# Holding three row loads back behind a transposing transfer, and rearranging one quad's rows on GpSimd

## The chip, the core and the metric

The kernel runs on one core of a Trainium2 chip. The core has TensorE (PE, matmuls), VectorE (DVE), ScalarE (ACT), GpSimd (POOL) and SyncE (SP), each with its own queue of instructions worked off in order, and 16 DMA engines that all queues of transfers share. The metric is device time in microseconds (us); lower is better. PSUM, where matmuls write, has eight banks.

## The reference

Two stages in one function. First an attention without softmax, for 8 batches, 12 heads, 448 positions and a head size of 64; then a two-layer perceptron over the 3584 rows of 768 that come out.

```
scores = q @ k^T / sqrt(64)
attn   = relu(scores)**2 / 448
x      = (attn @ v), heads side by side        # 3584 x 768
h      = x @ w_in                              # 768 x 2048
g      = max(h, 0) + alpha * min(h, 0)
out    = g @ w_out                             # 2048 x 768, float32
```

Inputs and output are float32. The kernel computes in bfloat16 with float32 sums.

## The kernel before, in words

**Tiling.** Four heads of one batch make a *quad*; there are 24, three to a batch. The 448 positions are laid out as 64 partitions by 7 chunks, and two heads share the 128 partitions. For each quad the kernel

- loads rows of q, k and v (`load_qk`, `load_v`), issued by GpSimd, which also turns float32 into bfloat16; 224 KB each as written;
- turns q and k so that the head size lies along partitions, into a tile `T`. Quads 0 to 4 do that on TensorE (`turn_pe`). From quad 5 on, `turn_dma` does: two copies rearrange the rows into a tile `perm` (L164), then SP issues a transposing transfer from `perm` to `T` (L166);
- computes scores per chunk (L178), relu on ScalarE (L187) or VectorE (L189), the square, mostly on VectorE (L197), and the product with v (`attnv`, L207), which ScalarE (L217) and VectorE (L218) scale into `xT`.

For each batch `f1` multiplies `xT` by w_in (L241, 16 blocks of 128 columns); ScalarE and VectorE apply the slope (L249, L250) into `gT`, which holds two batches. `f2` multiplies `gT` by w_out (L266) for one block of rows and either the first 256 or the last 512 columns, ScalarE copies the result out of PSUM (L268) and SP stores it (L274). `load_w_out(1)` loads w_out's last 512 columns in four quarters.

**Order.** All of it is written out by hand: each engine gets its instructions in the order in which the program makes the calls, and the framework adds the waits that the data needs. What matters around the change:

- *GpSimd's queue* issues all loads. At most eight of its transfers are under way, as they share eight semaphores. The stretch concerned, L374 to L380, is: rows of quad 6, q of quad 7, a 1x1 copy into `landed` that reads quad 5's `T` and so waits for its transposing transfer, k of quad 7, rows of quad 8, w_out's four quarters, v of quad 6.
- *SP's queue* issues the stores and the transposing transfers.
- *VectorE's queue* has the perm copies of quad 6 (`turn_dma(6)`, L389) after a run of squares and before the relu of quad 5's scores.
- *Buffers*: rows of q and of k, three each; `perm`, two; `T`, four; `gT`, one for two batches. Quads 5 and 7 use one `perm` buffer, 6 and 8 the other. Quad 9's rows come into the buffers of quad 6's.

After quad 4's scores TensorE's order is: `f2(0,0,0)`, scores of quad 4, `attnv(3)`, scores, `f2(0,1,0)`, `f2(0,2,0)`, scores of quad 5 (L396, the first readers of quad 5's `T`), `attnv(4)`, scores, then `f1` of batch 1 with `attnv(5)` inside it. Quad 6's scores come after `f1` of batch 1 and `f2(0,3,0)`.

Of the kernel before, what the change touches and what calls it, by code (L numbers as in the profile page):

```python
# [20 lines left out]
def kernel(  # L21
# [10 lines left out]
    nc = tc.nc  # L32
# [30 lines left out]
    landed = singles.tile([1, 1], BF16)  # L63
# [22 lines left out]
    def take_bank():  # L86
        i = min(range(8), key=lambda i: (taken[i], i))
        take(i, 1)
        return psum[:, i]


    raw, vraw = {}, {}

    def load_qk(n, names="qk"):
        b, g = divmod(n, NG)
        for name in names:
            src = q if name == "q" else k
            t = raw_pool.tile([128, 2, NJ, D], BF16, tag=name, name=f"{name}raw")
            flat = src[b].rearrange("(m two) (pp j) d -> (two pp) m (j d)", two=2, j=NJ)
            nc.gpsimd.dma_start(out=t.rearrange("p m j d -> p m (j d)"), in_=flat[:, 2 * g:2 * g + 2])  # L100
            raw[(n, name)] = t

    def load_v(n):
        b, g = divmod(n, NG)
        t = v_pool.tile([128, 2, NJ, D], BF16, tag="v", name="vraw")
        flat = v[b].rearrange("(m two) (pp j) d -> (two pp) m (j d)", two=2, j=NJ)
        nc.gpsimd.dma_start(out=t.rearrange("p m j d -> p m (j d)"), in_=flat[:, 2 * g:2 * g + 2])  # L107
        vraw[n] = t
# [11 lines left out]
    def load_w_out(h, lo=0, hi=KF, step=4):  # L120
        for lo in range(lo, hi, step):
            nc.gpsimd.dma_start(out=w_out_sb[h][:, lo:lo + step], in_=w_out_v[:, lo:lo + step, COLS[h][0]:COLS[h][1]])
# [24 lines left out]
    T = {}  # L147
# [10 lines left out]
            copy = nc.vector.tensor_copy if eng == "D" else nc.scalar.copy  # L158
            copy(dst, ps[:, 128 * lo:128 * hi])  # L159

    def turn_dma(n):
        p = perm_pool.tile([128, 2, NJ, 2, D], BF16, tag="perm", name="perm")
        for i, name in enumerate("qk"):
            nc.vector.tensor_copy(p[:, i], raw.pop((n, name)).rearrange("p s j d -> p j s d"))  # L164
        t = T_pool.tile([128, 2, NJ, 128], BF16, tag="T", name="T")
        nc.sync.dma_start_transpose(out=t.rearrange("p a j c -> p (a j) c"),  # L166
                                    in_=p.rearrange("p a j s d -> p (a j s d)"))
        T[n] = t
# [4 lines left out]
    def score_mm(n, j):  # L173
        ps = take_pair()
        t = T[n]
        for r in range(2):
            for c in range(2):
                nc.tensor.matmul(ps[64 * c:64 * c + 64, r, :S],  # L178
                                 t[64 * r:64 * r + 64, 1, j, 64 * c:64 * c + 64],
                                 t[64 * r:64 * r + 64, 0, :, 64 * c:64 * c + 64],  # L180
                                 start=True, stop=True)
        return ps

    def relu(ps, eng):
        rl = rl_pool.tile([128, 2, S], BF16, tag="rl", name="rl")
        if eng == "A":
            nc.scalar.activation(rl, ps[:, :, :S], ACTF.Relu)  # L187
        else:
            nc.vector.tensor_scalar(rl, ps[:, :, :S], 0.0, None, ALU.max)  # L189
        return rl  # L190
# [31 lines left out]
    def sc(chunks):  # L222

        for n, j, eng in chunks:
            late.append((n, j, relu(score_mm(n, j), eng)))

    def sq(k=99, eng="D"):
        for g in late[:k]:
            square(*g, eng)
        del late[:k]  # L230
# [28 lines left out]
    def f2(sb, c, h, parts=None):  # L259

        first_col, width = COLS[h][0], COLS[h][1] - COLS[h][0]
        o = o_pool.tile([128, d_model - CUT], F32, tag="o", name="osb")
        for lo, hi in parts or ((0, width),):
            ps = take_bank()[:, :hi - lo]
            for ff in range(KF):
                nc.tensor.matmul(ps, gT[sb][:, ff, bass.ts(c, 128)], w_out_sb[h][:, ff, lo:hi],  # L266
                                 start=(ff == 0), stop=(ff == KF - 1))
            nc.scalar.copy(o[:, lo:hi], ps)  # L268
            for u in range(2):
                blk = 2 * c + u  # L270
                b, j = 2 * sb + blk // NJ, blk % NJ
                rows = out[b * S:(b + 1) * S].rearrange("(pp j) d -> j pp d", j=NJ)
                eng = nc.scalar if u and parts else nc.sync
                eng.dma_start(out=rows[j][:, first_col + lo:first_col + hi], in_=o[64 * u:64 * u + 64, lo:hi])  # L274
# [4 lines left out]
    def ch(n, lo, hi, p=pat):  # L279
        return [(n, j, p[j]) for j in range(lo, hi)]  # L280
# [61 lines left out]
    def f1s(b, lo, hi):  # L342
        for ff in range(lo, hi):
            f1(b, ff)
# [6 lines left out]
    def prepare(n):  # L351
        if n < NQ:
            turn_dma(n)
        load(n + 2)
# [11 lines left out]
    f1s(0, 10, 12)  # L366
    sc(ch(3, 6, 7) + ch(4, 0, 2, "AA"))
    turn_dma(5)
    f1s(0, 12, 13)
    kept = late[:]  # L370
    del late[:]
    f1s(0, 13, 16)
    late += kept
    load_qk(6)  # L374
    load_qk(7, "q")
    nc.gpsimd.tensor_copy(landed, T[5][:1, 0, 0, :1])
    load_qk(7, "k")
    load_qk(8)
    load_w_out(1)
    load_v(6)  # L380
    f2(0, 0, 0)
# [4 lines left out]
    sq(3)  # L386
    sq(2, "A")
    sq()
    turn_dma(6)  # L389
    load_qk(9)  # L390
    load_v(7)
    load_v(8)
    load_v(9)
    f2(0, 1, 0)
    f2(0, 2, 0)
    sc(ch(5, 0, 3))  # L396
    sq(1)
    attnv(4)
# [117 lines left out]
```

## Time and profile before

| | |
|---|---|
| median of 7 runs | 386.25 us |
| lowest to highest | 386.09 to 387.46 us |
| the profiled execution | 387.46 us, of it 385.4 us span |
| PE busy | 375.3 us, 97% of the span |
| DVE busy | 266.4 us, 69% |
| ACT busy | 206.9 us, 54% |
| POOL busy | 67.9 us, 18% |
| transposing transfers, issue to landing | 19, median 6.6 us, 4.0 to 19.1 us |
| rows of q, issue to landing | 23, median 6.0 us |

The span runs from the first to the last instruction of the program in one profiled execution; the time is what the device reports around it. A busy share is of the span. A row of the timeline gives the start, the time from the first start to the last end of the merged instructions, the engine, the line of the kernel and the operation, what is written and read (`out<-in`) with partitions x elements, and in brackets how long the engine had been idle and what ended that. In a group's row the numbers after the bar are busy us, mean ns of one instruction and idle us just before. In the chain of waits each piece has its start, its length and what the time was spent on; a DMA's piece there is its whole flight. A row of DMA queues has packets, MB moved and the share of 16 engines' time. Engines named with a q (SPq) are seen while they issue.

### The profile page before, as it was taken

How to read it: one execution, taken by the hardware profiler on the slowest of the kernel's cores; microseconds unless marked ns; L12 is line 12 of the kernel's file. 1: busy time of each engine (PE TensorE's matmuls, PEld its weight loads, DVE VectorE, ACT ScalarE, POOL GpSimd, SP SyncE). 2: the span in 40 equal slices, each digit the busy share in tenths (PEclk: the TensorE clock that was granted, in tenths of full speed). 3: DMA queues.
4: the chain of work that ended last, by engine and by line, in shares of the span. 5: the costliest groups of instructions: out<-in, count | busy, mean ns of one | idle time of the engine just before them, and what ended most of it. 6: DMA issues, size and time to landing. Idle time of an engine off the chain costs nothing.

```text
span 385.4 us, 7838 instructions
## 1 busy us (share of the span) xinstructions
PE 375.3 (97%) x3178; PEld 205.9 (53%) x3200; DVE 266.4 (69%) x422; ACT 206.9 (54%) x331; POOL 67.9 (18%) x102
## 2 busy tenths in 40 slices
PE   7799999999999999999999999999999999999996
PEld 6444564555554455545465455544556445645554
DVE  3987987765768888689655897779855788526300
ACT  4977686545364664555445555637544375434321
POOL 7557325132202202022100222020000000000000
PEclk9999999999999999999999999999999999999999
DMA  9999999999992776698292972946036300120023
GB/s 159 187 204 196 201 122 212 180 194 225 177 190 47 114 129 94 111 143 110 54 161 57 146 122 42 174 66 123 21 78 95 77 0 16 43 68 2 14 68 84
DMA packets 73284, 43.42 MB, mean 113 GB/s; under 512 B 40352, under 2 KB 69792, under 8 KB 73248
## 3 DMA queue, kind: packets, MB, share of 16 engines
q0 software_dynamic: 26864, 22.45, 39.6%
q1 hardware_dynamic: 45952, 20.07, 26.8%
q8 instruction: 25, 0.41, 0.4%
q10 hardware_dynamic: 432, 0.39, 0.3%
q14 instruction: 11, 0.09, 0.1%
HBM read 45.62 MB, written 11.01 MB: 147 GB/s over the span
## 4 chain that ended last, share of the span: by engine, by line
PE 89%; DMA 6%; DVE 2%; issue 1%; ACT 0%; ACTq 0%; POOLq 0%
PE psum L266 37%; PE psum L241 36%; PE psum L178 9%; PE psum L207 7%; DMA T<-perm 3%; DMA kraw<-in_k_dram 2%; DMA qfirst<-in_q_dram 1%; DVE at L197 1%; PE psum L156 1%; DVE T L159 1%; DVE rl L189 1%; ACT osb L268 0%; ACTq L274 0%; DVE qraw L140 0%; POOLq L100 0%
## 5 line engine op out<-in xcount | busy, mean ns | idle before, releaser
L266 PE MATMUL psum<-w_out,gT 128*128 128x256 bf16 (+3 forms) x890 | 149.8, 322 | 1.2
L241 PE MATMUL psum<-xT,w_in_sb 128*128 128x448 bf16 x768 | 149.9, 353 | 0.0
L266 PEld LDWEIGHTS <-gT 128*128 128x128 bf16 x912 | 86.8, 98 | 64.2 <-issue 8.2
L241 PEld LDWEIGHTS <-w_in_sb 128*128 128x128 bf16 x768 | 73.5, 98 | 73.0 <-issue 5.5
L250 DVE SCALAR_TENSOR_TENSOR gT<-neg,beta_sb,psum 128x448 bf16<-128x448 f32 x128 | 83.6, 678 | 35.8 <-ACT neg L249 35.7
L249 ACT ACTIVATE neg<-psum 128x448 f32<-128x448 f32 x128 | 69.3, 547 | 61.4 <-PE psum L241 60.2
L187 ACT ACTIVATE rl<-psum 128x896 bf16<-128x896 f32 x113 | 97.9, 929 | 2.2 <-PE psum L178 2.2
L197 DVE TENSOR_TENSOR at<-rl 128x896 bf16<-128x896 bf16 x164 | 91.7, 619 | 0.0
L189 DVE TENSOR_SCALAR rl<-psum 128x896 bf16<-128x896 f32 x55 | 59.7, 1086 | 40.0 <-PE psum L178 39.9
L268 ACT COPY osb<-psum 128x256 f32<-128x256 f32 (+3 forms) x57 | 27.0, 473 | 104.4 <-PE psum L266 97.3
L178 PE MATMUL psum<-T 64*64 64x448 bf16 x672 | 44.7, 356 | 3.5 <-DVE T L159 1.3
L100 POOL DMA_DIRECT2D qraw<-in_q_dram x23 | 16.6, 721 | 156.9 <-DVE perm L164 148.4
L207 PE MATMUL psum<-at,vraw 64*64 64x448 bf16 x672 | 36.6, 350 | 0.3 <-DVE at L197 0.2
L178 PEld LDWEIGHTS <-T 64*64 64x64 bf16 x672 | 16.5, 106 | 22.2 <-issue 12.9
L207 PEld LDWEIGHTS <-vraw 64*64 64x64 bf16 x672 | 20.9, 106 | 12.6 <-issue 2.3
L218 DVE TENSOR_SCALAR xT<-psum 128x448 bf16<-128x448 f32 x23 | 14.4, 625 | 14.5 <-PE psum L207 10.9
L107 POOL DMA_DIRECT2D vraw<-in_v_dram x24 | 17.5, 729 | 7.5 <-DMA w_out<-in_moe_w_out_dram 4.3
L100 POOL DMA_DIRECT2D kraw<-in_k_dram x23 | 16.6, 722 | 6.4 <-DMA w_out<-in_moe_w_out_dram 3.4
L217 ACT ACTIVATE xT<-psum 128x448 bf16<-128x448 f32 x23 | 12.7, 550 | 2.6 <-PE psum L207 2.6
L164 DVE COPY perm<-qraw 128x896 bf16<-128x896 bf16 x19 | 11.7, 614 | 0.0
L164 DVE COPY perm<-kraw 128x896 bf16<-128x896 bf16 x19 | 11.6, 611 | 0.0
L117 POOL DMA_DIRECT2D w_in_sb<-in_moe_w_in_dram x16 | 10.1, 632 | 7.8 <-DMA qraw<-in_q_dram 2.3
(25 smaller groups left out, 41.9 us busy)
## 6 DMA issues: line engine op xcount, KB each, us to landing
out_dram<-osb SPq DMA_DIRECT2D x54, 128.0 KB, 2.4
vraw<-in_v_dram POOLq DMA_DIRECT2D x24, 224.0 KB, 8.1
qraw<-in_q_dram POOLq DMA_DIRECT2D x23, 224.0 KB, 6.0
kraw<-in_k_dram POOLq DMA_DIRECT2D x23, 224.0 KB, 7.1
out_dram<-osb SPq DMA_DIRECT2D x56, 64.0 KB, 2.2
w_in_sb<-in_moe_w_in_dram POOLq DMA_DIRECT2D x16, 192.0 KB, 9.0
w_out<-in_moe_w_out_dram POOLq DMA_DIRECT2D x4, 512.0 KB, 12.6
w_out<-in_moe_w_out_dram POOLq DMA_DIRECT2D x4, 256.0 KB, 8.9
```

The costliest lines, as they stand in the source:

```text
L100: nc.gpsimd.dma_start(out=t.rearrange("p m j d -> p m (j d)"), in_=flat[:, 2 * g:2 * g + 2])
L164: nc.vector.tensor_copy(p[:, i], raw.pop((n, name)).rearrange("p s j d -> p j s d"))
L178: nc.tensor.matmul(ps[64 * c:64 * c + 64, r, :S], t[64 * r:64 * r + 64, 1, j, 64 * c:64 * c + 64], t[64 * r:64 * r + 64, 0, :, 64 * c:64 * ...
L187: nc.scalar.activation(rl, ps[:, :, :S], ACTF.Relu)
L189: nc.vector.tensor_scalar(rl, ps[:, :, :S], 0.0, None, ALU.max)
L197: nc.vector.tensor_tensor(a, rl, rl, ALU.mult)
L207: nc.tensor.matmul(ps[64 * s:64 * s + 64, r, :S], vv[64 * r:64 * r + 64, s, j, :], a[64 * r:64 * r + 64, s], start=(j == 0), stop=(j == NJ ...
L241: nc.tensor.matmul(ps, w_in_sb[:, km // 2, km % 2, bass.ts(ff, 128)], xT[b][:, km // 2, km % 2, :], start=(km == 0), stop=(km == KM - 1))
L249: nc.scalar.activation(neg, ps, ACTF.Relu, scale=-1.0)
L250: nc.vector.scalar_tensor_tensor(gT[b // 2][:, ff, (b % 2) * S:(b % 2) * S + S], neg, beta_sb[:, ff:ff + 1], ps, ALU.mult, ALU.add)
L266: nc.tensor.matmul(ps, gT[sb][:, ff, bass.ts(c, 128)], w_out_sb[h][:, ff, lo:hi], start=(ff == 0), stop=(ff == KF - 1))
L268: nc.scalar.copy(o[:, lo:hi], ps)
```

## The change

The 1x1 copy that waits for quad 5's transposing transfer moves ahead of the rows of quad 6, so that the loads of q6, k6 and q7 wait too. The two copies that rearrange quad 6's rows go from VectorE to GpSimd, in its queue after the rows of quad 8 and before the four issues for w_out's last 512 columns. The issue of quad 6's transposing transfer on SP goes from before `f2(0,1,0)` to after `f2(0,2,0)`, so behind their four stores.

```diff
-    def turn_dma(n):
+    def rearrange_rows(n, eng):
         p = perm_pool.tile([128, 2, NJ, 2, D], BF16, tag="perm", name="perm")
         for i, name in enumerate("qk"):
-            nc.vector.tensor_copy(p[:, i], raw.pop((n, name)).rearrange("p s j d -> p j s d"))
+            eng.tensor_copy(p[:, i], raw.pop((n, name)).rearrange("p s j d -> p j s d"))
+        return p
+
+    def turn_dma(n, p=None):
+        p = p or rearrange_rows(n, nc.vector)
         t = T_pool.tile([128, 2, NJ, 128], BF16, tag="T", name="T")
...
     late += kept
+    nc.gpsimd.tensor_copy(landed, T[5][:1, 0, 0, :1])
     load_qk(6)
-    load_qk(7, "q")
-    nc.gpsimd.tensor_copy(landed, T[5][:1, 0, 0, :1])
-    load_qk(7, "k")
+    load_qk(7)
     load_qk(8)
+    rows6 = rearrange_rows(6, nc.gpsimd)
     load_w_out(1)
     load_v(6)
     f2(0, 0, 0)
...
     sq(2, "A")
     sq()
-    turn_dma(6)
     load_qk(9)
     load_v(7)
     load_v(8)
     load_v(9)
     f2(0, 1, 0)
     f2(0, 2, 0)
+    turn_dma(6, rows6)
     sc(ch(5, 0, 3))
```

## The prediction

> **What bounds the kernel now.** Times are us from the span's start; "T5" is the transposing transfer of quad 5, and so on; q6 and k6 are the row loads of quad 6. I read the page's chain first, then the chain in order of time, to find where TensorE isn't what ends last.
>
> ```profile
> PE 89%; DMA 6%; DVE 2%; issue 1%; ACT 0%; ACTq 0%; POOLq 0%
> ```
>
> ```profile
> 41.49 2.64 PE psum L241 x14
> 44.13 10.36 DMA T<-perm
> 54.49 0.04 issue
> 54.54 0.76 PE psum L178 x12
> ```
>
> TensorE sets the end. The chain leaves it at 44.13 for 10.36, the whole flight of T5, but that isn't what T5 costs: TensorE had other work meanwhile. Its own timeline has the price:
>
> ```profile
> 54.54 0.76 PE L178 MATMUL psum<-T 64*64 64x448 bf16 x12 [0.66 <-DMA T<-perm]
> ```
>
> It is idle from 53.88 to 54.54. After that no gap of it is longer than 0.05, so whatever is won or lost there reaches the end in full. GpSimd's timeline shows what T5 flew beside:
>
> ```profile
> 41.00 0.71 POOL L100 DMA_DIRECT2D qraw<-in_q_dram  x1 [0.83 <-PE psum L241]
> 42.13 0.71 POOL L100 DMA_DIRECT2D kraw<-in_k_dram  x1 [0.42 <-issue]
> 43.27 0.71 POOL L100 DMA_DIRECT2D qraw<-in_q_dram  x1 [0.43 <-issue]
> 54.55 0.18 POOL L376 COPY landed<-T 1x1 bf16<-1x1 bf16 x1 [10.57 <-DMA T<-perm]
> 55.03 0.72 POOL L100 DMA_DIRECT2D kraw<-in_k_dram  x1 [0.31 <-PE psum L178]
> ...
> 57.30 3.00 POOL L122 DMA_DIRECT2D w_out<-in_moe_w_out_dram  x4
> ```
>
> q6, k6 and q7 were issued just before T5; the last of them lands 10.2 after 43.27, at 53.5, and T5 at 54.5. VectorE's order just after matters for the moved copies:
>
> ```profile
> 56.24 0.61 DVE L197 TENSOR_TENSOR at<-rl 128x896 bf16<-128x896 bf16 x1
> 56.77 0.62 DVE L218 TENSOR_SCALAR xT<-psum 128x448 bf16<-128x448 f32 x1
> 57.31 1.08 DVE L189 TENSOR_SCALAR rl<-psum 128x896 bf16<-128x896 f32 x1
> 58.31 2.76 DVE L197 TENSOR_TENSOR at<-rl 128x896 bf16<-128x896 bf16 x5
> ```
>
> Here VectorE runs close ahead of TensorE. Half of quad 4's xT is ready at 57.39 and used by the fourth L241 matmul, at 56.94 + 3 x 0.2 = 57.54: 0.15 to spare. The fifth square ends at 61.07; quad 5's L207 matmuls start at 60.67 and reach it after five chunks of 0.2, at 61.67: 0.6 to spare.
>
> **What the Trainium skill says.** "SBUF — State Buffer", Who interferes with whom: GpSimd shares a pair of SBUF ports with VectorE, held for a whole instruction; a VectorE instruction with two SBUF inputs contends with a GpSimd one that reads SBUF, and who starts first makes the other wait. The squares (rl times rl) are of that kind, the L189 and L218 instructions, which read PSUM, are not. No row of before has GpSimd copying beside a square. "DMA: Bandwidth & Descriptors", Queues, rings and completion order: each DMA engine takes packets in turn from the queues that have work. The trace agrees for 76 to 82, where T7 flew beside loads, packet for packet:
>
> ```profile
> q0 software_dynamic: 1056, 0.89, 90.5%
> q1 hardware_dynamic: 1057, 0.27, 33.3%
> ```
>
> **The change, part by part.**
>
> *The three loads that now wait.* Without q6, k6 and q7 (3 x 229 KB as written, at the 201 GB/s of 36 to 50) queue 0 runs dry about 3.4 earlier. T5 then has the engines to itself sooner: 54.5 - 3.4 = 51.1; bounds 49.7 (issue 44.13 plus the 4.0 of the shortest transposing transfer, plus the rest of the older loads) and 52.5 (its slow pace when alone, 730 packets in 50.5 to 53, stays). TensorE asks at 53.88, so the wait goes: -0.66. Nothing sooner than 53.88 is to be had, TensorE is full there.
>
> *GpSimd's queue.* T5 lands at 51.3, say. Then the 1x1 copy and six issues (before: 0.48 to the first load, 0.72 to 0.85 each): 51.3 + 0.5 + 0.85 + 5 x 0.72 = 56.3. q6 lands 4.4 after its issue and k6 5.3 (q and k at 103.71 and 104.42, on idle engines): 56.2 and 57.95. So the copy of q starts at 56.3, that of k at 57.95. Their length isn't in the trace; the nearest rows:
>
> ```profile
> masks.py:199 POOL TENSOR_SCALAR_AFFINE_SELECT ident<-ident 128x128 bf16<-128x128 bf16 x1 | 0.3, 287 | 0.1
> masks.py:197 POOL MEMSET ident<- 128x128 bf16 x1 | 0.2, 204 | 0.3 <-POOLq L500 0.3
> ```
>
> Less the 93 to 95 ns of a 128x1 memset these are 0.87 and 1.5 ns per element of a partition; 896 elements on top of the 1x1 copy's 176 ns make 0.95 to 1.5, and I take 1.25. Upper bound 2.0, from the 4497 ns for 2048 elements that "GPSIMD Engine Reference", Performance versus the Vector engine, gives for a two-input add (an estimate; the same page calls one-input work nearly line-rate). The rows are done at 57.95 + 1.25 = 59.2. Behind them: w_out's four issues at 59.2 instead of 57.30. Its last quarter, issued 1.9 later, lands at 76.65 + 1.9 = 78.6 at worst (issue 59.52, 17.1 in flight before); the matmul that reads it runs at 79.80 + 12 x 0.216 - 0.66 = 81.7. Quad 9's rows, landed at 79.7 and 81.3, move to 83.2 at worst, read at 85.9. Both hidden; quads 7 and 8 land near 60 and 63 and are read at 64.6 and 72.3.
>
> *VectorE.* Two copies of 0.61 fewer, at 53.12 to 54.26. After them it waited 0.98 for TensorE, so: 0.
>
> *The shared ports.* Everything of TensorE and VectorE now runs 0.66 sooner: lone square 55.58 to 56.19, five squares from 57.65 to 60.41. The copy of q falls into the PSUM readers between. The copy of k meets the squares: if it gets between them, they end up to 1.25 later, less 0.6 to spare: 0.65. If the squares hold it off, it costs 0 and the rows come at 61.7. I take the middle: +0.3.
>
> *SP.* T6 goes behind four stores of 64 KB, issued in about 2.3 from 53.4 on, and waits for GpSimd: issue at 59.3 instead of 54.33. The stores lose T6's 1.53 ahead of them; nobody waits for them. First reader of T6: quad 6's scores, at 78.5. A nearer one: the two perm buffers alternate, so VectorE's copies for quad 8, at 72.3, need T6 landed. T6 at 59.3 has k8's tail ahead and w_out's issues beside and behind it. T11 and the like, issued between loads of the same moment, land in 6.3 (median of all 6.6): T6 at some 66 to 68. Cost: 0. T7 and T8 keep their places.
>
> Sum: -0.66 + 0.3 = -0.36. Against the profiled execution, 387.46 of which 385.4 is span, that is 387.1; I carry the difference to the median of the runs: 386.25 - 0.36 = 385.9. This kernel's runs tell about 0.2%, 0.77, from no change.
>
> **Rivals.**
>
> *The gain in full (faster).* GpSimd is held off or quick, and the T5 wait in an ordinary run is no shorter than in the profile. TensorE's idle 0.66, up to the 0.94 that its weight load waited for the same transfer: 385.3 to 385.6. Against it: the profiled run is the slowest of seven, so ordinary runs may have less of that wait.
>
> *Ports take more than T5 gives (slower).* With copies of 2.0 each, both starting ahead of squares, q is done at 58.3 and k at 60.3; the squares start 2.65 late, less 0.6: TensorE loses 2.05, net +1.4: 387.6. If T5 lands 0.7 sooner, the copy of q hits the lone square, and xT with it: up to 1.85 lost after 0.15 to spare, +1.2. It decides from copies of 1.7 each: 56.3 + 3.4 - 57.65 - 0.6 = 1.45 lost, against 0.66 won.
>
> *T6 late (slower).* If T6 shares packet for packet with w_out, as T7 did (16.5) and T8 (19.1), it lands at 75.8 or 78.4. VectorE's quad 8 copies wait, and five L250 instructions behind them (1.05 + 5 x 0.61 + 0.07 = 4.2) feed the last matmul of the next L266 group, due at 78.4: free up to a landing at 74.1, then one for one. 75.8: +1.7 - 0.36, so 387.6. Speaking for it: w_out's megabytes start at the same moment. Against: T7 and T8 met a backlog of eight loads, T6 meets the tail of one.
>
> **How the numbers follow.** Forecast 0.38 (its own range 385.4 to 386.9), full gain 0.26, ports 0.20, T6 late 0.16. The forecast lies within 0.2% but for 0.04 on the faster side: faster 0.30, same 0.34, slower 0.36. The range runs from the full gain, 385.2, to 387.8, leaving out T6 landing as late as T8 did and less than 0.1 on the fast side.
>
> **What would show it.** T5 landing by 52.5 and no idle time ahead of the first L178 after 53.8; GpSimd's two copies at 1.0 to 1.5 each; the squares after them no more than 1.25 late; T6 landed by 70 and no wait ahead of quad 8's perm copy. Wrong, if T5 isn't earlier without the three loads (its slow stretch may be its own, then the gain is 0 and the later issues stay), if a copy takes over 1.7, or if VectorE stands still near 72.

## The result, and the profile after

| | before | after |
|---|---|---|
| median | 386.31 us (35 runs, 385.78 to 387.55) | 388.26 us (14 runs, 387.17 to 389.17) |
| the profiled execution, of it span | 387.46, 385.4 | 388.61, 386.7 |

The ratio after to before is 1.0043, interval 1.0034 to 1.0053: about 1.7 us slower. The forecast was 385.9 and the range ended at 387.8; the changed kernel lies above it. It went the way of the rival "T6 late", near its price (387.6). Here and below, ratios and intervals are of runs in the faster state; one run of each of two kernels, at 392.2 and 392.3, is left out of them as over 1.5% above its kernel's fastest.

**Where the time stands now.** The page's chain of the kernel after has 3 points less of TensorE than before, one more of transfers and two more of VectorE:

```profile
PE 86%; DMA 7%; DVE 4%; issue 1%; POOL 0%; ACT 0%; ACTq 0%; DVEq 0%
```

The chain in order of time says which transfer. T5 has left it; T6 stands there with 18.32, and behind it VectorE's work comes on the path:

```profile
56.13 0.94 POOL perm L164
57.08 0.02 issue
57.09 18.32 DMA T<-perm
75.41 0.03 issue
...
75.53 1.15 DVE perm L164 x2
76.68 1.89 DVE gT L254 x4
...
78.96 0.69 DVE gT L254
79.64 0.05 issue
79.69 0.28 PE psum L270
```

(The lines of the kernel after count four higher than before's from L166 on: L254 was L250, L270 was L266.) In words: GpSimd ends the copy of k at 57.07, SP issues T6 at 57.09, T6 lands at 75.41, and only then can VectorE write quad 8's rows into the `perm` buffer that T6 read.

**The first half went better than forecast.** GpSimd's timeline after:

```profile
49.48 0.18 POOL L378 COPY landed<-T 1x1 bf16<-1x1 bf16 x1 [10.51 <-DMA T<-perm]
49.97 0.72 POOL L100 DMA_DIRECT2D qraw<-in_q_dram  x1 [0.30 <-PE psum L182]
...
54.24 0.97 POOL L164 COPY perm<-qraw 128x896 bf16<-128x896 bf16 x1
56.13 0.93 POOL L164 COPY perm<-kraw 128x896 bf16<-128x896 bf16 x1 [0.92 <-DMA kraw<-in_k_dram]
57.01 2.98 POOL L122 DMA_DIRECT2D w_out<-in_moe_w_out_dram  x4
```

T5, issued at 44.05, landed at 49.42 (it was 54.5), the two copies took 0.97 and 0.93, and w_out's issues begin at 57.01, no later than the 57.30 of before. TensorE and VectorE just after, after:

```profile
53.66 0.76 PE L182 MATMUL psum<-T 64*64 64x448 bf16 x12
```

```profile
55.37 0.62 DVE L201 TENSOR_TENSOR at<-rl 128x896 bf16<-128x896 bf16 x1
55.90 0.62 DVE L222 TENSOR_SCALAR xT<-psum 128x448 bf16<-128x448 f32 x1
56.43 1.08 DVE L193 TENSOR_SCALAR rl<-psum 128x896 bf16<-128x896 f32 x1
57.43 2.76 DVE L201 TENSOR_TENSOR at<-rl 128x896 bf16<-128x896 bf16 x5
```

No bracket ahead of the first L182 now: TensorE doesn't wait for T5. The lone square takes 0.62 and the five take 2.76, as before: GpSimd's copies, at 54.24 to 55.21 and 56.13 to 57.06, overlap VectorE's PSUM readers and not the squares.

**The second half lost it.** VectorE's timeline at quad 8's copies, first before, without a wait, then after:

```profile
72.97 0.61 DVE L164 COPY perm<-qraw 128x896 bf16<-128x896 bf16 x1
```

```profile
71.50 0.68 DVE L254 SCALAR_TENSOR_TENSOR gT<-neg,beta_sb,psum 128x448 bf16<-128x448 f32 x1 [0.45 <-ACT neg L253]
75.53 0.62 DVE L164 COPY perm<-qraw 128x896 bf16<-128x896 bf16 x1 [3.36 <-DMA T<-perm]
76.07 0.61 DVE L164 COPY perm<-kraw 128x896 bf16<-128x896 bf16 x1
76.59 3.04 DVE L254 SCALAR_TENSOR_TENSOR gT<-neg,beta_sb,psum 128x448 bf16<-128x448 f32 x5
```

VectorE stands still for 3.36. The five L254 behind it run back to back and deliver `gT` late, which TensorE's timeline and its weight loads' waits show:

```profile
76.39 1.80 PE L270 MATMUL psum<-w_out,gT 128*128 128x256 bf16 x13
78.51 0.28 PE L270 MATMUL psum<-w_out,gT 128*128 128x256 bf16 x1 [0.31 <-DVE gT L254]
79.10 0.28 PE L270 MATMUL psum<-w_out,gT 128*128 128x256 bf16 x1 [0.31 <-DVE gT L254]
79.69 0.28 PE L270 MATMUL psum<-w_out,gT 128*128 128x256 bf16 x1 [0.31 <-DVE gT L254]
79.91 0.76 PE L182 MATMUL psum<-T 64*64 64x448 bf16 x12
```

```profile
PEld L270 <- DVE gT L254: 1.8, 4, 0.5
```

From its first matmul to the scores after it this group took 79.91 - 76.39 = 3.52. Before, its 16 matmuls ran through, in 79.11 - 77.27 = 1.84:

```profile
77.27 1.91 PE L266 MATMUL psum<-w_out,gT 128*128 128x256 bf16 x16
79.11 0.76 PE L178 MATMUL psum<-T 64*64 64x448 bf16 x12
```

So TensorE came in 0.88 ahead (T5's wait of 0.66 is part of that) and left 0.80 behind: 1.68 lost in one place. The brackets add to 0.93 only; the rest isn't shown as idle time because the matmuls' ends are modelled, but the weight loads' 1.8 agree with it.

Both kernels were profiled once more side by side, in ordinary executions: spans of 384.1 and 386.2. Those two are compared below as "before again" and "after again".

### The profile page after: what moved, and what is told of

It is laid out like the page before. It is cut to its first block, busy times and chain, and to the rows that moved or that the text cites. A ratio compares the mean times of both kernels' runs of the same rounds, so it can differ in the third digit from the quotient of the medians.

```text
span 386.7 us, 7837 instructions
## 1 busy us (share of the span) xinstructions
PE 375.1 (97%) x3178; PEld 205.5 (53%) x3200; DVE 265.1 (69%) x420; ACT 206.9 (53%) x331; POOL 69.7 (18%) x104
## 4 chain that ended last, share of the span: by engine, by line
PE 86%; DMA 7%; DVE 4%; issue 1%; POOL 0%; ACT 0%; ACTq 0%; DVEq 0%
PE psum L270 36%; PE psum L245 33%; PE psum L182 8%; PE psum L211 7%; DMA T<-perm 5%; DVE at L201 2%; DMA kraw<-in_k_dram 1%; DMA qfirst<-in_q_dram 1%; PE psum L156 1%; DVE gT L254 1%; DVE T L159 1%; DVE rl L193 1%; DVE perm L164 0%; POOL perm L164 0%; ACT osb L272 0%
## 5 line engine op out<-in xcount | busy, mean ns | idle before, releaser
L270 PE MATMUL psum<-w_out,gT 128*128 128x256 bf16 (+3 forms) x890 | 150.5, 322 | 2.1 <-DVE gT L254 0.9
L245 PE MATMUL psum<-xT,w_in_sb 128*128 128x448 bf16 x768 | 149.9, 353 | 0.0
L270 PEld LDWEIGHTS <-gT 128*128 128x128 bf16 x912 | 86.7, 98 | 66.0 <-issue 8.2
L245 PEld LDWEIGHTS <-w_in_sb 128*128 128x128 bf16 x768 | 73.6, 98 | 73.0 <-issue 5.5
L254 DVE SCALAR_TENSOR_TENSOR gT<-neg,beta_sb,psum 128x448 bf16<-128x448 f32 x128 | 83.3, 678 | 34.1 <-ACT neg L253 34.0
L182 PE MATMUL psum<-T 64*64 64x448 bf16 x672 | 44.7, 356 | 3.0 <-DVE T L159 1.1
L182 PEld LDWEIGHTS <-T 64*64 64x64 bf16 x672 | 16.6, 106 | 21.4 <-issue 12.9
```

Source lines behind the costliest of these rows:

```text
L182: nc.tensor.matmul(ps[64 * c:64 * c + 64, r, :S], t[64 * r:64 * r + 64, 1, j, 64 * c:64 * c + 64], t[64 * r:64 * r + 64, 0, :, 64 * c:64 * ...
L245: nc.tensor.matmul(ps, w_in_sb[:, km // 2, km % 2, bass.ts(ff, 128)], xT[b][:, km // 2, km % 2, :], start=(km == 0), stop=(km == KM - 1))
L254: nc.vector.scalar_tensor_tensor(gT[b // 2][:, ff, (b % 2) * S:(b % 2) * S + S], neg, beta_sb[:, ff:ff + 1], ps, ALU.mult, ALU.add)
```

## The experiments

The theory after the result: T6, issued beside w_out's loads, lands late, and what this costs is paid at the second `perm` buffer; T5's gain is there but small. Rivals: the shared SBUF ports, the later start of the loads, and something outside this stretch.

### Before and after again

No edit; one profile each.

> The kernel before once more, for a second profile. If the T5 wait of 0.66 belongs to every execution: TensorE idle 0.6 to 0.7 again ahead of quad 5's scores and a span near 385.4. If the first profile caught a long one: T5 lands before 53.9, no idle time there, span near 384.1, which is what the ordinary executions beside the last runs had.

> The changed kernel once more, for a second profile. Theory T6-late: T6 lands between 74 and 77, VectorE's quad 8 copies wait 2.5 to 5, TensorE loses 0.6 to 3 in the L270 group that follows. If it lands before 73.5 and nothing waits, the loss of the first profile was chance and another cause is needed.

386.12 and 388.2. TensorE's timeline of before again has the wait that the forecast put at 0.66:

```profile
53.22 0.76 PE L178 MATMUL psum<-T 64*64 64x448 bf16 x12 [0.23 <-DMA T<-perm]
```

It is 0.23 here: the first profile was of the slowest of its seven runs. After again repeats the loss (T6 issued at 57.46, landed at 75.08; quad 8's copies waited 3.35; three gaps of 0.31). There GpSimd's copy of k, later by 0.4, met the first of the five squares, which took 2.93 together instead of 2.76; TensorE lost nothing by it. Comparing the two by where time passes, with the start taken up to the scores after the first long wait (TensorE's gap of 0.88 that ends at 11.28 and 11.71), and the tail from TensorE's last end to the end of the span:

| | before again | after again | difference |
|---|---|---|---|
| start | 11.28 | 11.71 | +0.43 |
| body | 369.23 | 370.59 | +1.36 |
| tail | 3.57 | 3.91 | +0.34 |
| span | 384.08 | 386.21 | +2.13 |

In after again the L270 group took 3.50 up to the scores, in before again 1.84: 1.66 lost. With -0.23 for T5 that makes +1.43, and the body's +1.36 agrees. The other 0.77 lies at the two ends of the span, far from quads 5 to 8; it comes up again below.

### A third perm buffer

```diff
-    perm_pool = ctx.enter_context(tc.tile_pool(name="perm", bufs=2))
+    perm_pool = ctx.enter_context(tc.tile_pool(name="perm", bufs=3))
```

> The changed kernel with three perm buffers instead of two, nothing else. Theory T6-late (quad 6's transposing transfer lands at 75.4 and VectorE's copies for quad 8 wait for its buffer, 3.4 us): the wait ahead of the quad 8 copies goes to 0, T6 still lands near 75, the 1.7 us that TensorE loses in the L270 group at 76 to 80 are won back, and the time is that of before less the 0.66 that T5 gave: 385.6 or so, ratio to before 0.998. Theory ports (GpSimd's copies slow VectorE) or theory loads (w_out and what follows come too late): nothing changes, ratio stays at 1.004.

386.55 beside 386.08; ratio 1.0012, interval 1.0006 to 1.0019. T6 is as late as ever (57.57 to 75.91), but VectorE's timeline shows quad 8's copies going ahead 4 us before it lands:

```profile
71.19 0.68 DVE L254 SCALAR_TENSOR_TENSOR gT<-neg,beta_sb,psum 128x448 bf16<-128x448 f32 x1 [0.46 <-ACT neg L253]
71.79 0.61 DVE L164 COPY perm<-qraw 128x896 bf16<-128x896 bf16 x1
72.31 0.61 DVE L164 COPY perm<-kraw 128x896 bf16<-128x896 bf16 x1
72.84 1.30 DVE L254 SCALAR_TENSOR_TENSOR gT<-neg,beta_sb,psum 128x448 bf16<-128x448 f32 x2
```

TensorE has no idle time over 0.06 from 20 to the end. The body is 384.55 - 11.71 - 3.90 = 368.94, 1.65 shorter than that of after again and 0.29 shorter than that of before again. So the late landing costs only through the buffer. Of the loss, 1.0043 to 1.0012 is gone, 1.2 us by the ratios and 1.7 by the medians. The 385.6 that was expected did not come: what stays over before is the subject of the last experiment.

### Quad 8's copies later

```diff
-        if ff in (1, 10):
+        if ff in (1, KF - 1):
             turn_dma(7 + ff // 9)
```

Two buffers, as after; quad 8's copies and T8's issue come behind the last L254 of this `f1`.

> The changed kernel with VectorE's copies for quad 8 moved from after the eleventh to after the last L254 instruction of batch 1; two perm buffers as before. Theory T6-late: the copies may still wait for T6, but nothing that TensorE needs soon stands behind them, so the L270 group runs through; T8 has to follow T7 anyway (85 in the profile of the changed kernel). Time as with three buffers: ratio 0.999 to 1.002. If the loss has another cause: 1.004 stays.

386.49 beside 386.1; ratio 1.0010, interval 1.0004 to 1.0017. T6 lands at 75.11, the copies come at 77.22 without a wait, TensorE has no gap over 0.06, the body is 368.98. T8 lands at 96.69, and nothing waits for it. That it gives the same as the third buffer, without one, shows that the price was the five L254 queued behind the waiting copies, not the late T6 or T8.

### w_out behind T6

```diff
     rows6 = rearrange_rows(6, nc.gpsimd)
-    load_w_out(1)
-    load_v(6)
...
     turn_dma(6, rows6)
+    nc.gpsimd.tensor_copy(landed, T[6][:1, 0, 0, :1])
+    load_w_out(1)
+    load_v(6)
```

The loads that GpSimd issues behind v of quad 6 (quad 9's rows and v of quads 7 to 9) stay behind it, so they are held back too.

> The changed kernel with a second 1x1 copy on GpSimd that waits for T6, and w_out's last 512 columns, v of quad 6 and all later loads issued after it. If T6 is late because it takes turns with w_out's packets, it now lands within 6 to 9 us of its issue at 57.1, by 66, and the quad 8 copies do not wait. If T6 is slow by itself or by its place on SP, it lands near 75 as before. What comes of the time is open: w_out is issued 8 us later, its first quarter is read at 79, so that wait may come in place of the other: ratio 0.998 to 1.010.

387.27 (11 runs, 386.31 to 392.32); ratio 1.0036, interval 1.0013 to 1.0059. T6 is issued at 57.09, to the hundredth as in after, behind the same rows of quads 7 and 8 and the same four stores, and lands at 63.84: 6.8 in flight instead of 18.3. So w_out, with the loads behind it, is why T6 was late. The queues, first of after from 60 to 75, then of this kernel from 58 to 64:

```profile
q0 software_dynamic: 2156, 2.11, 91.1%
q1 hardware_dynamic: 1959, 0.55, 34.8%
```

```profile
q1 hardware_dynamic: 2039, 0.63, 69.3%
q0 software_dynamic: 452, 0.37, 39.0%
T<-perm SPq DMA_TRANSPOSE x1, 6.8
```

Beside w_out each queue got about as many packets (2156 and 1959), but w_out's are larger and take 91.1% of the engines' time. Without it T6's queue sends as many packets, 2039, in 6 us instead of 15. (Both windows have some packets of other transfers in the same queue.) The Trainium skill, "DMA: Bandwidth & Descriptors", Queues, rings and completion order, states that an engine takes packets in turn from the queues that have work, and the equal counts agree; the rival used it, the forecast didn't.

The gain is given back at once. TensorE's timeline of this kernel:

```profile
78.47 2.76 PE L270 MATMUL psum<-w_out,gT 128*128 128x512 bf16 x12
82.15 1.02 PE L270 MATMUL psum<-w_out,gT 128*128 128x512 bf16 x4 [0.92 <-DMA w_out<-in_moe_w_out_dram]
```

w_out's last quarter, issued at 66.64, is now what comes too late. T6 and w_out want the same engines in the same 20 us, and with T6 issued as late as 57 neither of the two orders served both in time; the two experiments before this one let T6 be late instead. Two of the eleven runs, at 392.1 and 392.3, had a mean granted clock of 0.991; no trace of one was taken.

### Each part of the change alone

Only the wait moved, against before (rows rearranged by VectorE, T6 issued at its old place in SP's queue):

```diff
+    nc.gpsimd.tensor_copy(landed, T[5][:1, 0, 0, :1])
     load_qk(6)
-    load_qk(7, "q")
-    nc.gpsimd.tensor_copy(landed, T[5][:1, 0, 0, :1])
-    load_qk(7, "k")
+    load_qk(7)
```

> The kernel before with the wait for T5 ahead of the rows of quads 6 and 7, nothing else: quad 6's copies stay on VectorE, ahead of a relu of quad 5. k6 lands near 56 (56.1 in the changed kernel), so VectorE stands from 53 to 56 plus its own 1.1 and the relu, square and xT of quad 4 are some 3 late: TensorE loses 2.5 to 3.5 near 56 to 60. T6 is issued near 57.3, so it is as late as in the changed kernel and the quad 8 copies wait too. Ratio 1.007 to 1.014. If GpSimd's part of the change were what costs, this would be no slower than 1.004.

389.64 (4 runs, 388.38 to 390.48); ratio 1.0081, interval 1.0061 to 1.0101. T5 lands at 49.40, but VectorE, which must now wait for q6 (1.35) and k6 (1.93) in front of quad 5's relu, holds TensorE up for 2.69. So the move to GpSimd is no ornament: the moved wait needs it. T6, issued at 56.91, flew for 16.5 here as well; quad 8's copies, expected to wait for it, didn't, for with everything later by then they came at 75.99 and T6 had landed at 73.37.

Only the rows moved to GpSimd (this diff is against after, with the wait back at its old place):

```diff
-    nc.gpsimd.tensor_copy(landed, T[5][:1, 0, 0, :1])
     load_qk(6)
-    load_qk(7)
+    load_qk(7, "q")
+    nc.gpsimd.tensor_copy(landed, T[5][:1, 0, 0, :1])
+    load_qk(7, "k")
```

> The changed kernel with the wait for T5 back at its old place (q6, k6 and q7 ahead of it): only GpSimd's copies and the later issue of T6 are left of the change. T5 lands at 54.5 again and TensorE waits 0.66. GpSimd's copies come after k8's issue, from 57.3, beside VectorE's five squares (58.3 to 61.1). Theory T6-late: T6 is issued near 59.3 and lands at 75 to 78, the quad 8 copies wait 2 to 5 us, TensorE loses 1 to 4 us in the L270 group: ratio 1.004 to 1.012. Theory ports: the squares are 1 to 2 us longer together, or GpSimd's copies are, and TensorE waits ahead of quad 5's L211 group. If neither: ratio 1.000.

390.41 (4 runs, 388.74 to 390.77); ratio 1.0113, interval 1.0098 to 1.0128. T6 is issued at 58.10 and lands at 75.72, and quad 8's copies wait 3.32. T5 was expected at 54.5 with 0.66 of waiting; it landed at 53.03 and nothing waited for it, nor in the next kernel (53.12). With the same three loads ahead of it T5 thus flew for 10.4, 9.9, 9.3 and 9.4 in four profiles, and TensorE waited 0.66, 0.23, 0 and 0: that wait differs from execution to execution. Then VectorE, GpSimd and TensorE disturb each other:

```profile
55.05 1.35 DVE L201 TENSOR_TENSOR at<-rl 128x896 bf16<-128x896 bf16 x1
```

```profile
55.85 1.34 POOL L164 COPY perm<-qraw 128x896 bf16<-128x896 bf16 x1
```

```profile
56.99 1.11 PE L245 MATMUL psum<-xT,w_in_sb 128*128 128x448 bf16 x5 [0.51 <-DVE xT L222]
```

A square of 1.35 and a copy of 1.34, instead of 0.62 and 0.94, with xT late by more than its 0.15 of slack and 0.51 lost on TensorE. It looks like the meeting that the prediction feared, but that is inferred: by these rows a square of 0.62 would have ended at 55.67, 0.18 before the copy began, and times on GpSimd are rough.

The same with three perm buffers:

> The rows-only kernel (GpSimd rearranges quad 6's rows, T5's wait at its old place: 1.0113) with a third perm buffer. It can no longer lose at quad 8's copies, so what stays over before is the copies and squares that contend for the ports, and T5's wait. Theory (the two losses add up: 1.6 at the copies of quad 8, 0.5 at the squares): 1.6 us under rows-only, some 388.7 beside a before of 386.1, the squares again stretched from 0.61 to over 1. Rival (contention is most of it): within 0.5 us of rows-only, 390. Rival (contention costs nothing that lasts): within 0.5 us of before.

386.84 (20 runs); ratio 1.0014, interval 1.0008 to 1.0021. This is the third of the expected outcomes, nearly: 3.6 us went with the buffer, over twice what the theory of two adding losses gave, and what is left is within 0.65 us of before. In this profile GpSimd's first copy begins at 55.93, after the square's end at 55.68; the second, from 56.81 to 57.74, stretches the five squares to 3.23 (2.76 without), and TensorE loses nothing by it, since they had 0.6 to spare. So what GpSimd's copies cost is a matter of the moment: 0.51 at the lone square, nothing at the five.

Why rows-only lost 2 us more in three of its four runs (spans 388.4 to 389.0) than in its profile (386.9) goes with the granted clock: it averaged 0.994 to 0.995 in those runs and 0.999 in the profiled one. No trace of such a run of this kernel was taken. The kernel with only the wait moved, whose profile is of such a run (0.996), shows what such a loss looks like. Its windows have the stretch, its length, TensorE's busy time and matmuls, the granted clock, the transfers' share and GB/s:

```profile
50.00:55.00 5.00, 5.00 (x72) 1.00 0.79 98
55.00:58.00 3.00, 0.31 (x9) 1.00 1.18 170
58.00:60.00 2.00, 1.99 (x10) 0.75 1.24 195
60.00:62.00 2.00, 2.00 (x12) 0.50 1.21 198
62.00:64.00 2.00, 2.00 (x16) 0.89 1.22 196
```

TensorE stands still for 2.69. In windows of half a microsecond its clock is 0.50 from 59.0 to 62.4 and 1.00 on both sides: 3.4 us at half rate, 1.7 lost, beginning 1.1 after it was back at work. By their mean clock of 0.996 two of this kernel's four runs have it (spans of 388.3 and 388.4) and two don't (386.4 and 387.0). The Trainium skill, "TensorE: Matmul & The Clock Gate", Part 1, describes such a gate: half rate after an idle window of about 3.4 us, windows that run on whatever the kernel does. The half rate agrees, and that only some runs are struck fits windows that run on; the idle time doesn't agree: 2.69 was enough here.

In their profiles rows-only and its three-buffer form are 2.3 apart in the body (371.23 and 368.93): 1.64 at quad 8's copies, 0.51 at the square. Of the 3.6 between the medians 1.3 are left, and 387 x 0.004 = 1.5 is what the lower mean clock would cost. That rows-only's gaps of 0.51 and three times 0.31 bring the clock down is inferred from the averages, not seen in a trace.

### Only q7 behind the wait

Before, with one load fewer ahead of T5:

```diff
     load_qk(6)
-    load_qk(7, "q")
     nc.gpsimd.tensor_copy(landed, T[5][:1, 0, 0, :1])
-    load_qk(7, "k")
+    load_qk(7)
```

> The kernel before, with only q of quad 7 moved behind the wait for T5; rows of quad 6 stay early, copies stay on VectorE, T6 stays where it was. T5 should land 1.1 to 1.3 us sooner, at 53.2 to 53.4, ahead of 53.88: TensorE's idle 0.66 goes and nothing else is late. If the T5 wait is in ordinary runs what it is in the profiled one: ratio 0.998, time 385.6. If ordinary runs have less of it, 0.999 to 1.000.

387.2 (22 runs, 385.77 to 392.19); ratio 1.0037, interval 1.0019 to 1.0054. In its profile (span 383.8, the shortest of all) T5 lands at 52.14 and TensorE waits for nothing; but the ordinary runs spread over 6 us. A second profile caught one of the long ones:

> A second profile of before with q7 alone behind T5's wait, whose ordinary times spread from 385.8 to 392.2 while its profile stood at a span of 383.8. If the spread comes from w_out or T6 landing late, this profile, should it be one of the slow ones, shows TensorE waiting for w_out near 81 or VectorE waiting for T6 near 72, by over 0.5. If it comes from TensorE's granted clock alone, the gaps are as in the first and the matmuls are longer.

388.45, span 386.5. TensorE's timeline:

```profile
82.73 1.02 PE L266 MATMUL psum<-w_out,gT 128*128 128x512 bf16 x4 [1.35 <-DMA w_out<-in_moe_w_out_dram]
```

T6, issued at 53.88, took 16.1 this time (in the first profile of this kernel 11.7, in before again 6.4, both issued at 53.45), and w_out's last quarter landed 1.35 after its reader asked. Another wait of 0.58, at 108.16, followed. The four stores of 64 KB took 11.4 (median) instead of before's 6.1. GpSimd wasn't late: w_out's issues begin at 55.24, in before again at 55.99. It was the flights that were longer. The edit puts 229 KB more into the stretch where T6 and w_out fly, and in one of its two profiles they came through in time; why they were so much slower in the other was not found. It isn't all of the spread either: the four longest runs, 389.9 to 392.2, had a mean granted clock of 0.991 to 0.996, and no trace of one was taken.

### What is left without T6's cost

Four kernels without the wait at quad 8's copies stand at 1.0010 to 1.0014, though their bodies are 0.1 to 0.3 shorter than before's. To see whether this comes with where the instructions lie, quad-8-later was run with the 1x1 copy made twice:

```diff
     nc.gpsimd.tensor_copy(landed, T[5][:1, 0, 0, :1])
+    nc.gpsimd.tensor_copy(landed, T[5][:1, 0, 0, :1])
```

> As the kernel with quad 8's copies later, with the 1x1 copy that waits for T5 made twice: one GpSimd instruction of some 0.18 us more, of no use, and every later instruction of GpSimd a place further on. The kernel without it had a body (from the first quad's ramp to TensorE's last matmul) 0.29 shorter than before's and was still at 1.0010 of before, because the start took 0.15 and the last two stores 0.33 longer. If those two have nothing to do with the edits but with where the program's instructions happen to lie, they may come out otherwise here: the last stores land 1.8 and 2.05 after their issue, and the time is 0.2 to 0.4 under before (0.9990 to 0.9995). If they come with the moved rows, they land 2.2 and 2.4 after it, and the time is again 0.3 to 0.5 over (1.0008 to 1.0013).

386.79 beside 386.19; ratio 1.0013, interval 1.0006 to 1.0019; the last two stores landed 2.20 and 2.40 after issue. That one edit of place changed nothing. Two pieces can be told apart, the start and the tail:

*The start* differs between executions of one kernel. TensorE's first rows in before and in before again:

```profile
5.59 0.96 PE L156 MATMUL psum<-ident,qraw 128*64 128x128 bf16 x14 [0.21 <-DVE qraw L140]
```

```profile
5.43 0.58 PE L156 MATMUL psum<-ident,qraw 128*64 128x128 bf16 x14 [0.40 <-DVE qraw L140]
```

The same 14 matmuls of one kernel took 0.96 and 0.58. Seven of the thirteen profiles have the long form: two of the five of before and its variants, five of the eight with rows on GpSimd. Where it is short, the start mostly ends at 11.3, where it is long, at 11.7, so it is worth about 0.4 us in a comparison of two single profiles. It looks like a clock that comes up sooner or later, but the granted clock reads 1.00 from 4.5 to 6.5 in both, and the latest start of all, 12.03 in after, has the short form: the cause is open.

*The tail* goes with the kernel: 3.56 to 3.57 in all five profiles of before and its variants, 3.90 to 4.07 in seven of the eight profiles in which GpSimd rearranges rows, where the last two 32 KB stores land 2.2 to 2.6 after their issue instead of 1.8 to 2.05. The exception is the kernel with w_out behind T6, which has the short tail. Why stores at 382 should feel an edit at 55 is open.

Body and tail together put the four kernels 0.04 to 0.28 over before again. Their medians are 0.39 to 0.65 over before's, so some 0.3 to 0.45 more has no explanation; whether rows on GpSimd make the long start more frequent can't be told from thirteen profiles.

No version beats before: T5's wait was 0.23 in the one ordinary run of before that was profiled, under what these runs can tell, and every kernel without it stands at 1.0010 or above.

## Why the prediction was wrong

*T5 and the three loads.* Right in kind, too careful in size: it landed at 49.42, just outside the bounds of 49.7 to 52.5, and nothing waited. The flight took 5.4, and 5.4 to 6.1 in all seven profiles where the three loads wait, against 9.3 to 10.4 in the four where they don't.

*The gain of 0.66.* Mis-sized: 0.23 in before again, and nothing in two profiles of other kernels with the same loads ahead of T5. The rival for the full gain named the reason itself, that the profiled run was the slowest of seven, and the forecast took the 0.66 nevertheless.

*GpSimd's copies.* 1.25 was taken from a range of 0.95 to 1.5; they took 0.93 to 0.98 in every profile, but for the one of 1.34 in rows-only. With T5 earlier too, rows were done at 57.07 instead of 59.2, and w_out's issues didn't move. Right that it was hidden.

*The shared ports.* +0.3 was taken for the five squares, 0 was paid in the changed kernel: the copies fell between the squares, by luck of the moment, and where one met the five squares (2.84 to 3.23 together in four profiles) the 0.6 of slack held. The lone square, which only the rival on the ports considered, did cost in other kernels: besides the 0.51 of rows-only, it took 0.95 and 0.91 in w_out-behind-T6 and in the kernel with two 1x1 copies, and the eight L245 that read its xT took 1.95 and 1.91 instead of 1.69.

*T6: the step that failed.* "T11 and the like, issued between loads of the same moment, land in 6.3 (median of all 6.6): T6 at some 66 to 68. Cost: 0." Issued at 57.09, 2.2 sooner than the forecast had it, it landed at 75.41 and cost about 1.7. The median of 19 transfers was used for one that leaves 0.1 us after 2 MB of w_out begin to be issued; the fitting rows were T7, which flew beside the second half of w_out, and T8, beside the loads that followed, for 16.5 and 19.1. The argument against the rival, that T7 and T8 met a backlog of eight loads, doesn't hold: of loads T6 met the last of quad 7's and quad 8's rows, which had all landed by 62.3, and what w_out and the loads behind it added was enough, as holding them back showed (6.8 in flight). The rival had the place and the chain of five L250 right. Its size, +1.7, was meant for a landing at 75.8; at 75.41 its rule (free up to 74.1, then one for one) gives 1.3, so that it comes so near is in part luck. Its chance of 0.16 was too low.

*The sum.* -0.23 (T5) + 1.66 (T6) + 0 (ports) gives +1.43, and the body's difference is 1.36. The rest of the difference between the two single profiles, 0.77, is the start and the tail's stores, which no step of the prediction had.

## What to carry to other kernels

When a transfer is moved to a later issue, price its flight by the transfers that fly beside the same neighbours, not by the median of its kind; here the difference was 6.8 to 18.3 us. Then ask who waits for its *source* buffer, not only for its result: T6's reader, at 79.9 in after, never had to wait, the writer of its two-deep buffer did, and a third buffer or a later place for the next writer took the cost away. A wait read from one profile is to be held against how that execution stands among the runs before it is counted as gain: T5's was 0.66, 0.23, 0 and 0 in four profiles.

## What the runs showed that was not expected

- A stall of TensorE of 2.69 us was followed, 1.1 us after it was over, by 3.4 us at half of its clock: 1.7 more, over half as much again. It was seen in one trace; by its mean clock a second of the four runs had it too.
- The lone square, where it starts inside a GpSimd copy, ended 0.49 after the copy did (copy to 55.10, square to 55.59; copy to 55.48, square to 55.97; likewise 0.49 with three buffers and with quad 8's copies later), so most of its 0.62 seems to come after it. The Trainium skill, "SBUF — State Buffer", Who interferes with whom, says that who starts first makes the other wait; this agrees. In rows-only, where the square started first, both were longer (1.35 for 0.62, 1.34 for 0.94), and that rule alone doesn't give it.
- Moving a single 229 KB load by some 10 us widened the spread of the runs from before's 1.4 us (50 runs beside it) to 6.4, or to 5.0 without the longest.
- GpSimd's copy of 128x896 in bf16 takes 0.93 to 0.98, only half as long again as VectorE's 0.61.
